# Scaling P on GpSimd ahead of its transpose, swapping the halves of q on GpSimd, and one pool of four 2-bank PSUM tiles

## Chip, cores and metric

The kernel runs on one core of one Trainium2 chip. The metric is the device time of one execution in microseconds (us); lower is better. Before the change it took 650.79 us, the median of 4 runs (650.27 to 651.2).

## The reference, cut to what matters

```python
B, H, S, D = 8, 8, 576, 64
scores = q @ k.T / sqrt(D)                       # per batch and head, 576 x 576
thresh = max(scores, axis=-1) - tau              # tau = 0.02
scores = where(scores >= thresh, scores, -1e9)
attn   = exp(scores - max);  attn /= sum(attn) + 1e-9
x      = (attn @ v) as (B*S, H*D)                # 4608 x 512
h      = max(x @ w1, x @ w2, x @ w3)             # 4608 x 768
out    = h @ w_out                               # 4608 x 512
```

## The kernel before

Work goes in *quads* of four heads, two quads to a batch, 16 in all. A quad is nine *steps*; a step makes two score tiles of 128 queries by 576 keys. In steps 1, 4 and 7 of a quad, counted from 0, the threshold is applied on VectorE, in the others on ScalarE. P is transposed by DMA, and the products for a quad are made in the next quad. Where a batch is complete, its feed-forward is cut into pieces that are slipped between later steps.

```python
ps_s = tc.tile_pool(name="ps_s", bufs=3, space=PSUM)   # 2 banks each: scores, transposes, products
ps_f = tc.tile_pool(name="ps_f", bufs=2, space=PSUM)   # 1 bank each: feed-forward
...
# q transposed; every second use needs it with its two halves of 64 rows swapped:
nc.scalar.activation(out=t, in_=ps[:, 192:768], func=AF.Copy, scale=scale)
nc.gpsimd.dma_start(out=s[0:64], in_=t[64:128])
nc.gpsimd.dma_start(out=s[64:128], in_=t[0:64])
...
def scores(L, idx):                    # both tiles of a step, one after the other
    for i in (1, 0):
        ps = slot("sc")
        for r in (0, 1):               # row half r of the array, its own PSUM bank
            # key columns: i=1: 256 (r=0) and 320 (r=1);  i=0: 320 and 256
            nc.tensor.matmul(ps[:, cols], t[rows, off:off+128], L["kt", pr][rows, kc], ...)
...
def softmax(L, idx, sc):
    nm = -max(sc) (VectorE);  bm = nm + tau
    z  = Exp(sc + nm)  or  Prelu(sc + bm)              # ScalarE, reads PSUM
    P  = z * (z >= thr) (VectorE)  or  Exp(z) (ScalarE), with the row sums
    dma_start_transpose(pt, P)
...
def sums(L):                           # 1/sum of a quad: transpose, DRAM, broadcast back
def product(L, pr, xt):                # P @ v, then times 1/sum on VectorE
def hid(f, a):                         # 3 x 4 matmuls of 288 columns, each evacuated 288 wide
...
for idx in range(9):                   # a step
    fin = softmax(L, idx, sc)
    sc = scores(next step)
    side(g, idx)                       # sums, products, transposes of the next quad's q and k
    if todo: todo.pop(0)()             # one feed-forward piece
    fin()
    if wl and idx >= 2: wl.pop(0)()    # weight loads, in quad 0
```

## Time and profile before

| | before |
|---|---|
| time, median | 650.79 us |
| TensorE (PE) busy | 568.4 us, 87% |
| VectorE (DVE), ScalarE (ACT), GpSimd (POOL) busy | 65%, 60%, 16% |
| first maximum of a score tile | 34.8 us |
| a batch in the steady stretch | 71.4 us |
| from the last reciprocal of the sums to the end | 47.8 us |

The lines of this profile are in the prediction below. In a row of the timeline, the brackets give how long the engine was idle just before and what ended the wait. A chain row gives a start, a length and what took the time.

### The profile page before, as it was taken

What the parts mean: (1) busy time and instruction counts of PE and PEld (TensorE: products, weight loads), DVE (VectorE), ACT (ScalarE), POOL (GpSimd) and SP (SyncE); (2) the same over time, 40 slices, a digit from 0 to 9 for tenths busy, and PEclk for the clock granted to TensorE, in tenths of its full rate; (3) what the DMA queues carried; (4) which work ended last, traced back from release to release, by engine and by line L of the source; (5) the groups of instructions that cost most, each with busy time, mean ns of one, the idle gap of its engine ahead of it and who ended that gap; (6) DMA issues with size and microseconds to landing.
All of it is one profiled execution on the core that took longest, in us unless ns stands there. A gap on an engine that the chain in (4) does not pass through costs nothing.

```text
span 651.5 us, 10435 instructions
## 1 busy us (share of the span) xinstructions
PE 568.4 (87%) x3634; PEld 311.4 (48%) x3648; DVE 423.1 (65%) x880; ACT 389.8 (60%) x841; POOL 105.3 (16%) x194
## 2 busy tenths in 40 slices
PE   3178786999989999999989998999989898999696
PEld 1034333455536553555445553556455553655363
DVE  0055567687667876787767876788668776786141
ACT  1046566666766758576667667675765676676122
POOL 1300111111221012111121112101211021100201
PEclk9999979899999999999999999999999999999899
DMA  8985769776796979796987779685958769574402
GB/s 217 259 196 103 168 143 205 153 172 144 170 220 156 168 132 252 145 190 138 200 198 167 129 171 232 131 197 128 240 124 169 106 112 198 100 121 74 127 1 74
DMA packets 220661, 103.09 MB, mean 158 GB/s; under 512 B 187184, under 2 KB 214208, under 8 KB 220608
## 3 DMA queue, kind: packets, MB, share of 16 engines
q1 hardware_dynamic: 209152, 70.80, 54.7%
q0 software_dynamic: 11456, 31.62, 18.8%
q8 instruction: 29, 0.48, 0.3%
q14 instruction: 24, 0.20, 0.1%
HBM read 44.04 MB, written 9.58 MB: 82 GB/s over the span
## 4 chain that ended last, share of the span: by engine, by line
PE 43%; ACT 24%; DVE 17%; issue 7%; DMA 6%; POOL 0%; SPq 0%; ACTq 0%; POOLq 0%; DVEq 0%
PE sc L155 15%; PE ph L257 13%; ACT P L193 8%; ACT z L182 8%; DVE nm L173 8%; PE tp L124 7%; PE o L232 5%; DVE P L190 4%; DMA qs<-qt 2%; PE po L268 2%; ACT z L180 2%; DMA rb<-rd 2%; ACT qt L128 2%; ACT ob L271 2%; DMA vm<-in_v_dram 2%
## 5 line engine op out<-in xcount | busy, mean ns | idle before, releaser
L173 DVE TENSOR_REDUCE nm<-sc 128x1 f32<-128x576 f32 x288 | 208.6, 752 | 100.3 <-PE sc L155 82.3
L155 PE MATMUL sc<-kt,qs 64*128 64x256 f32 (+1 forms) x512 | 188.9, 473 | 39.4 <-ACT z L182 22.6
L182 ACT ACTIVATE z<-sc,bm 128x576 f32<-128x576 f32 x192 | 134.0, 742 | 122.5 <-DVE bm L176 105.7
L257 PE MATMUL ph<-xt,w 128*128 128x288 bf16 x1152 | 178.1, 289 | 15.2 <-DVE xt L237 5.3
L155 PE MATMUL sc<-kt,qt 64*128 64x256 f32 (+1 forms) x512 | 181.8, 467 | 5.0 <-ACT qt L128 3.0
L257 PEld LDWEIGHTS <-w 128*128 128x128 bf16 x1152 | 107.5, 98 | 77.9 <-issue 49.9
L193 ACT ACTIVATE P<-z 128x576 bf16<-128x576 f32 x192 | 130.0, 690 | 0.0
L155 PEld LDWEIGHTS sc<-kt,qs 64*128 64x128 f32 x512 | 84.6, 197 | 72.9 <-ACT z L182 38.7
L155 PEld LDWEIGHTS sc<-kt,qt 64*128 64x128 f32 x512 | 86.4, 197 | 45.8 <-issue 22.2
L190 DVE SCALAR_TENSOR_TENSOR P<-z 128x576 bf16<-128x576 f32 x96 | 71.4, 753 | 24.8 <-ACT z L180 24.8
L128 ACT ACTIVATE qt<-tp 128x576 f32<-128x576 f32 x32 | 20.8, 651 | 79.8 <-PE tp L124 79.8
L260 ACT ACTIVATE hm<-ph 128x288 bf16<-128x288 f32 x96 | 39.7, 413 | 47.6 <-PE ph L257 47.6
L180 ACT ACTIVATE z<-sc,nm 128x576 f32<-128x576 f32 x96 | 67.2, 751 | 0.0
L262 DVE TENSOR_TENSOR hm<-ph,hm 128x288 bf16<-128x288 f32 x96 | 43.7, 455 | 34.3 <-ACT hm L260 24.6
L268 PE MATMUL po<-wo,hT 128*128 128x512 bf16 (+1 forms) x226 | 56.9, 380 | 1.2 <-ACT ob L271 0.4
L262 DVE TENSOR_TENSOR hT<-ph,hm 128x288 bf16<-128x288 f32 x96 | 43.9, 457 | 13.2 <-PE ph L257 9.2
L130 POOL DMA_DIRECT2D qs<-qt x32 | 16.8, 527 | 195.8 <-ACT hm L260 119.7
L232 PE MATMUL o<-ptq,vb 128*64 128x288 bf16 (+2 forms) x512 | 45.5, 301 | 2.3 <-ACT z L182 2.0
L112 POOL CAST vb<-vm 128x1024 bf16<-128x1024 f32 x16 | 16.7, 1042 | 145.6 <-issue 114.9
L193 ACT ACTIVATION_READ_ACCUMULATOR P<-z 128x1 f32 x192 | 40.0, 208 | 0.0
L274 POOL DMA_DIRECT2D out_dram<-ob x40 | 22.4, 560 | 107.8 <-ACT ob L271 107.5
L134 DVE COPY kt<-tp 128x576 f32<-128x576 f32 x32 | 24.1, 754 | 18.3 <-PE tp L124 18.2
(39 smaller groups left out, 396.9 us busy)
## 6 DMA issues: line engine op xcount, KB each, us to landing
qs<-qt POOLq DMA_DIRECT2D x64, 144.0 KB, 3.3
rb<-rd POOLq DMA_DIRECT2D x32, 288.0 KB, 4.7
qm<-in_q_dram SPq DMA_DIRECT2D x16, 512.0 KB, 5.3
km<-in_k_dram SPq DMA_DIRECT2D x16, 512.0 KB, 5.2
vm<-in_v_dram SPq DMA_DIRECT2D x16, 512.0 KB, 4.2
out_dram<-ob POOLq DMA_DIRECT2D x32, 256.0 KB, 3.8
w<-in_moe_w_dram POOLq DMA_DIRECT2D x3, 768.0 KB, 10.8
ptq<-P SPq DMA_TRANSPOSE x144, 3.4
```

Of the source, the lines that this page charges most:

```text
L124: nc.tensor.transpose(ps[:, col:col + np_], src.rearrange("p a d -> p (a d)"), identf[:np_, :np_])
L155: nc.tensor.matmul(ps[:, cols], t[rows, off:off + 128], L["kt", pr][rows, kc], start=True, stop=True)
L173: nc.vector.tensor_reduce(out=nm[:, n:n + 1], in_=sc[n], axis=AX, op=OP.max, negate=True)
L180: nc.scalar.activation(out=zn, in_=sc[n], func=AF.Exp, bias=nm[:, n:n + 1])
L182: nc.scalar.activation(out=zn, in_=sc[n], func=AF.Prelu, bias=bm[:, n:n + 1], alpha=-STEEP)
L190: nc.vector.scalar_tensor_tensor(out=pn, in0=zn, scalar=thr, in1=zn, op0=OP.is_ge, op1=OP.mult, accum_out=acc)
L193: nc.scalar.activation(out=pn, in_=zn, func=AF.Exp, accum_out=acc)
L232: nc.tensor.matmul(ps[64 * i:64 * i + 64, first + a:first + e], w, x, start=(m == 0), stop=(m == 4))
L257: nc.tensor.matmul(ps[:, :n], wts[wi][:, kc, f * 128:(f + 1) * 128], xt[:, kc, cols], start=(kc == 0), stop=(kc == 3))
L260: nc.scalar.activation(out=hm, in_=ps[:, :n], func=AF.Copy)
L262: nc.vector.tensor_tensor(out=hm if wi == 1 else hT[:, f, cols], in0=ps[:, :n], in1=hm, op=OP.max)
L268: nc.tensor.matmul(ps[:r, :], hT[:, f, c * 128:c * 128 + r], wo[:, f, :], start=(f == 0), stop=(f == NF - 1))
```

## The change

Its intent: (1) multiply P by 1/sum before it is transposed, on idle GpSimd, so that sums need no trip through DRAM; (2) swap the halves of q by GpSimd copies instead of transfers; (3) one pool of four 2-bank PSUM slots for everything, score tiles and other pieces in turn, and the hidden pieces evacuated 576 wide. Weight loads are cut up and begin later in quad 0, the first input loads are split, and outputs leave over the sync queue. The change also gives z a fourth buffer, casts v later, and keeps GpSimd's instructions in the order in which they are written.

```diff
-    ps_s = ctx.enter_context(tc.tile_pool(name="ps_s", bufs=3, space=PSUM))
-    ps_f = ctx.enter_context(tc.tile_pool(name="ps_f", bufs=2, space=PSUM))
+    ps_s = ctx.enter_context(tc.tile_pool(name="ps_s", bufs=4, space=PSUM))
...
-            nc.gpsimd.dma_start(out=s[0:64], in_=t[64:128])
-            nc.gpsimd.dma_start(out=s[64:128], in_=t[0:64])
+            pool.tensor_copy(out=s[0:64], in_=t[64:128])
+            pool.tensor_copy(out=s[64:128], in_=t[0:64])
...
+    def normalized(L, idx, z, sm):
+        rs = small.tile([128, 2], F32, name="rs")
+        vector.reciprocal(rs, sm)
         P = pp.tile([128, W], BF16, name="P")
+        for n in range(2):
+            pool.tensor_scalar(out=P[:, n * S:(n + 1) * S], in0=z[:, n * S:(n + 1) * S],
+                               scalar1=rs[:, n:n + 1], scalar2=1.0, op0=OP.mult, op1=OP.mult)
+        nc.sync.dma_start_transpose(out=L["pt"][:, :, idx * 128:(idx + 1) * 128], in_=P)
-    def sums(L):
...                                     (trip through DRAM, and the multiply in product, removed)
-        def hid(f, a):                  # 12 matmuls, three 1-bank tiles
+        def hid(f, wi):                 # 8 matmuls, one 2-bank tile, evacuated 576 wide
...
-        for idx in range(9):            # two score tiles, then the rest
+        for per in range(18):           # one score tile, one other piece
+            idx, i = per // 2, 1 - per % 2
+            exponents(L, idx, i, sc)
+            sc = scores(next tile)
+            ...
+            other(g, per)               # product at 3 and 8, q/k transposes at 10, 12, 14, 16,
+                                        # else a feed-forward piece
+            if wl and (g or per >= 6) and per % 2:
+                wl.pop(0)()             # weights in 18 loads, from period 7 of quad 0
```

## The prediction

> **What bounds the kernel now.** Words first: a *batch* is two *quads* of four heads; a quad is nine steps; a step makes two score tiles of 128x576 and takes maximum, exponent, threshold and sum of each. Each pair of quads is followed by the feed-forward of its batch, cut into pieces between later steps. I read the page's busy line, then the busy table by stage, then the chain that ended last, then the PE timeline of one steady stretch, then the groups.
>
> The page says TensorE is the busy engine:
>
> ```profile
> PE 568.4 (87%) x3634; PEld 311.4 (48%) x3648; DVE 423.1 (65%) x880; ACT 389.8 (60%) x841; POOL 105.3 (16%) x194
> ```
>
> So GpSimd (POOL) is nearly free, and 83 us of 651.5 have no matmul. The stages tell where. The reciprocal-sum transposes (rp, rs) mark quad starts, at 74.7, 106.8 and 139.06; the first maximum is at 34.8 us. Columns: stretch, length, then busy us of PE, PEld, DVE, ACT, POOL, then clock, DMA share, GB/s.
>
> ```profile
> 34.80:74.70 39.90, 30.74 (x109) 15.41 (x108) 21.92 (x43) 23.30 (x49) 3.36 (x6) 1.00 0.68 148
> 74.70:106.83 32.13, 24.25 (x143) 11.75 (x141) 21.45 (x43) 20.41 (x43) 4.93 (x9) 0.89 0.76 165
> 106.83:139.06 32.23, 28.40 (x184) 14.97 (x184) 22.50 (x48) 20.74 (x46) 4.93 (x9) 0.89 0.76 160
> 139.06:603.20 464.14, 438.09 (x2954) 242.59 (x2965) 342.72 (x717) 312.73 (x681) 77.51 (x141) 1.00 0.77 162
> 603.20:651.50 48.30, 36.52 (x224) 20.64 (x223) 13.02 (x29) 10.02 (x22) 5.96 (x11) 0.90 0.21 64
> ```
>
> The time is 34.8 (start) + 39.9 + 32.1 + 32.2 (quads 0, 1, 2) + 464.1 (13 quads of 35.7) + 48.3 (end) = 651.4. Only the 464 us stretch is TensorE's, at 94% busy. The chain shows what holds start and end (start us, length, what):
>
> ```profile
> 17.55 14.89 DMA qs<-qt
> ...
> 59.37 2.29 PE sc L155 x8
> ...
> 128.77 1.17 PE sc L155 x8
> ...
> 606.44 2.32 DMA rd<-rT
> ...
> 609.56 4.66 DMA rb<-rd
> ...
> 644.63 0.61 ACT ob L271
> ```
>
> At the start everything waits 15 us for the half-swapped q (qs), a transfer queued among weight and input loads. At the end the 1/sum goes through DRAM (rd, rb), and 6.2 us still follow the copy of an output piece (ob). The same eight score records take 2.29 us in quad 0 and 1.17 later: TensorE starts at half rate. In the steady stretch the gaps have this form:
>
> ```profile
> 326.11 0.53 PE L155 MATMUL sc<-kt,qs 64*128 64x320 f32 x1 [0.91 <-ACT z L182]
> ...
> 337.33 0.70 PE L155 MATMUL sc<-kt,qs 64*128 64x256 f32 x2 [1.02 <-ACT z L182]
> ```
>
> A score matmul waits until ScalarE has read an older tile: three PSUM slots serve scores, transposes and products.
>
> **What the Trainium skill says.** *TensorE: Matmul & The Clock Gate*, Part 1: the array runs at half clock until an activity window of about 3.4 us is busy, and falls back after an idle one; Part 4: transposes do not count as that activity. The trace agrees: 2.29 against 1.17 us, and 57 to 66 us, dense with alternating scores and transposes, stayed slow, while dense scores from 75.0 to 78.4 were followed by full rate. *GPSIMD Engine Reference*, section 3.1: a one-input loop with at most two operations costs about 1.03 cycles an element at 1.2 GHz. The casts agree:
>
> ```profile
> L112 POOL CAST vb<-vm 128x1024 bf16<-128x1024 f32 x16 | 16.7, 1042 | 145.6 <-issue 114.9
> ...
> L113 POOL CAST vrb<-vr 128x128 bf16<-128x128 f32 x16 | 4.8, 301 | 0.0
> ```
>
> (1042-301)/896 = 0.83 ns an element plus 195 ns. *SBUF — State Buffer*, "Who interferes with whom": a VectorE instruction with two SBUF inputs contends with a GpSimd instruction that reads SBUF. That is the masked threshold (L190, 96 of 753 ns, both inputs z); with GpSimd this idle, the trace cannot show it yet.
>
> **The change, part by part.**
>
> *TensorE.* Its work stays, less the 16 rp transposes. From dense runs of the chain and timeline: a step's scores 1.17 us, four transposes with remainder 0.95, a product 1.71, twelve hidden matmuls 1.82, an output piece 1.46. Per batch 18x1.17 + 8x0.95 + 4x1.71 + 12x1.82 + 5x1.46 = 64.7 us, 32.4 a quad. The steady quad takes 35.7, so at most 3.3 a quad, 43 us in 13 quads, can be won.
>
> *Steady quads.* Now 18 periods a quad, each one score tile and one other piece, in turn, over four 2-bank slots. A score slot is reused after two periods, 2x1.80 = 3.6 us at TensorE's pace. A tile needs 0.58 to be written, 0.75 maximum (L173), 0.17 bias, 0.74 exponent, some 0.15 of handovers: 2.4. So 1.2 us are left for queueing on VectorE and ScalarE, whose single pieces block for about 0.67 us. Periods with a transpose (0.58+0.95, twice 3.06) leave 0.66. Most gaps of 0.9 to 1.0 should close; short ones remain, above all in masked steps, where a period holds maximum, threshold and often an evacuation on VectorE, 3x0.67 = 2.0 us against 1.8. I choose to win half of the 3.3: 34.0 a quad, 442 us, a gain of 22.
>
> *VectorE.* 192 feed-forward maxima of 0.456 become 96 of about 0.75 (-15.6); bias 96 to 192 (+13.5); 144 reciprocals at 0.2 for 16 (+24.5); rT and the 512-wide scaled copy go (-4.3, -10.9): net +7, some 430 us, 26.5 a quad, below 32.4. *ScalarE.* 96 copies of 0.413 become 48 of 0.74 (-4), 16 copies of 0.6 added (+9.6): some 395, 24.7 a quad. *GpSimd.* 288 scalings of 576 at 0.195+0.83x0.576 = 0.67 us (193), 64 swap copies at 0.67 (43), casts 21.5, 18 weight issues at 0.85 (15): 273 us, 17 a quad. Scaling adds about 1.7 us ahead of each transpose; only the end feels it, as the products run 3 and 8 periods into the next quad.
>
> *Start.* No weight load, no qs transfer; loads split so the first two heads land first. Eight issues of about 0.6 us on the queue, 1.15 MB at 200 to 250 GB/s: the last k at about 8 us, its transposes to 9.6, first tile to 10.9, first maximum at about 12 (was 34.8): gain 23.
>
> *Quads 0 and 1.* Without feed-forward they are held by the other engines and by latency. Pipelined records of ScalarE cost 0.63 each (chain), so an unmasked tile costs 1.30 on ScalarE, a masked one 1.42 on VectorE: 12x1.30 + 6x1.42 = 24.1 a quad if nothing overlaps. At half rate TensorE needs 9x2.29 + 4x1.54 = 26.8 in quad 0. I take 26.5 (was 39.9) and, with products and perhaps some slow clock, 27 (was 32.1). Quad 2, half with feed-forward: 9x1.5 + 9x1.87 = 30.3 (was 32.2). Gain 20.
>
> *End.* From the last exponents to the first hidden matmul: reciprocal 0.2, scaling 1.4, transpose about 3.5, second product 1.7, copy 0.8, about 7.6 us, instead of 11.6 (603.6 to 615.2); less cold ramp (5.30 for 24 matmuls where later 3.65); last output issued by the sync queue. 48.3 becomes 42.5.
>
> Sum: 12 + 26.5 + 27 + 30.3 + 442 + 42.5 = 580.3.
>
> **The rivals.** (a) *The slots give nothing*: the shared pool puts feed-forward pieces, which had two banks of their own, into the scores' queue, and the in-order engines pass one wait to the next. For it: VectorE and ScalarE are at 82% and 76% of such a pace. Against: before, three slots served scores in twos. Steady quads stay 35.7: 602 us. (b) *GpSimd is slower than a cast*: two per-partition scalars, or port contention with L190. At 1.2 us a scaling it has 27 us a quad, still hidden; only beyond 1.6 us does it pass TensorE. At 2 us, 16x40 us and the ends: over 690. Only copies and casts are measured here, so I keep a few per cent. (c) *The clock stays slow through quads 0 and 1*: then TensorE needs 27 and 33 us: some 8 us more, 588. (d) *The steady quads reach TensorE's 32.4*: 560.
>
> **Range and chances.** The start and end gains (23 and 6) rest on transfers seen on the chain and are nearly sure; 29 us alone is 4.5%. Quads 0 to 2 give 8 to 25, steady quads -5 to 43. Outer values 560 and 608. Faster by over 2% needs under 637.8: only rival (b), or a wait I do not see, prevents it.
>
> **What would show each step.** Right: first maximum near 12 us; quad pace 33 to 35; TensorE over 95% busy in the steady stretch, gaps before score matmuls mostly under 0.5 us; scalings of 0.6 to 1.1 us; no qs, rd, rb transfer; hidden matmuls 8 us after the last exponent. Wrong: GpSimd over 80% busy or named as releaser of transposes and products; L190's successor well over 0.75 us; score matmuls still waiting about 1 us for exponents; quads 0 or 1 over 32 us at 2.29 a step.

## The result, and the profile after

The changed kernel took **575.19 us** (median of 4 runs, 570.12 to 576.84) against 650.79 (650.27 to 651.2); the ratio is 0.883 (95% interval 0.878 to 0.888). Here and below a ratio is the mean time of one kernel's fast runs over that of the other's in the same rounds, so it is not quite the ratio of the medians quoted. The profiled run spans 568.3 us and belongs to the fastest of the four.

The page's busy line of the changed kernel:

```profile
PE 541.7 (95%) x3619; PEld 280.1 (49%) x3632; DVE 429.6 (76%) x976; ACT 415.8 (73%) x809; POOL 316.0 (56%) x408
```

TensorE's busy time is down by 27 us, its idle time from 83 to 27 us. The busy table by stage (columns as in the prediction), cut at the first maximum and then at the last reciprocal of the sums of quads 0, 1, 2 and 15:

```profile
0.00:12.20 12.20, 8.20 (x30) 5.30 (x32) 1.52 (x2) 2.58 (x3) 3.36 (x10) 1.00 0.70 199
12.20:36.92 24.72, 19.11 (x108) 8.56 (x106) 22.29 (x57) 21.74 (x45) 18.30 (x24) 1.00 1.05 219
36.92:67.30 30.38, 22.99 (x140) 11.78 (x140) 22.00 (x56) 22.32 (x46) 27.04 (x38) 0.83 1.19 239
67.30:95.89 28.59, 25.45 (x173) 13.26 (x174) 23.06 (x57) 23.52 (x48) 21.68 (x30) 0.94 0.95 192
95.89:533.85 437.96, 436.97 (x2953) 221.87 (x2964) 350.45 (x794) 336.67 (x656) 244.14 (x306) 1.00 0.68 139
533.85:568.30 34.45, 29.02 (x219) 19.32 (x219) 10.24 (x15) 9.02 (x15) 1.47 (x2) 0.98 0.24 74
```

| stretch, us | before | predicted | after |
|---|---|---|---|
| to the first maximum | 34.8 | 12 | 12.2 |
| quad 0 | 39.9 | 26.5 | 24.7 |
| quad 1 | 32.1 | 27 | 30.4 |
| quad 2 | 32.2 | 30.3 | 28.6 |
| 13 steady quads | 464.1 | 442 | 438.0 |
| end | 48.3 | 42.5 | 34.4 |
| sum | 651.4 | 580.3 | 568.3 |

(Before is cut as in the prediction, whose cuts are not of one kind: 74.7 and 106.83 are transposes of 1/sum, 139.06 is the end of a reciprocal, and 603.2 lies 0.5 us before the last one. Cut at the reciprocals, like the changed kernel, before has 37.5, 32.8, 33.7, 464.9 and 47.8. Where experiments are compared below, a quad is measured from its first maximum to the next quad's: quads 0 and 1 then last 34.4 and 33.4 us before, 22.7 and 30.4 after. The clock column counts as full any time for which the trace has no clock record: it says 1.00 up to 12.2 us, where eight score records take 2.31 us, half rate.)

In the steady stretch TensorE now idles for 1.0 us in 438. Its timeline, in which each group of score records (sc) is followed by eight hidden matmuls (ph), and no row carries a wait in brackets:

```profile
231.23 0.48 PE L172 MATMUL sc<-kt,qs 64*128 64x256 f32 x1
231.24 0.53 PE L172 MATMUL sc<-kt,qt 64*128 64x320 f32 x1
231.55 0.38 PE L172 MATMUL sc<-kt,qs 64*128 64x256 f32 x1
231.61 0.43 PE L172 MATMUL sc<-kt,qt 64*128 64x320 f32 x1
231.97 1.15 PE L259 MATMUL ph<-xt,w 128*128 128x288 bf16 x8
233.06 0.53 PE L172 MATMUL sc<-kt,qs 64*128 64x320 f32 x1
```

A single tile runs from 231.23 to 231.97, 0.74 us, then a piece of 1.09: a period of 1.83 us.

The chain at the start:

```profile
4.62 3.65 DMA km<-in_k_dram
8.32 1.60 PE tp L143 x5
9.92 2.31 PE sc L172 x8
12.23 1.41 DVE nm L190 x2
```

and at the end:

```profile
535.67 3.27 DMA ptq<-P
...
538.98 0.85 PE o L236 x10
539.83 17.77 PE ph L259 x144
...
557.87 6.34 PE po L272 x28
```

The k loads end the wait at the start, and no swap stands between transposes and scores. At the end all 144 hidden matmuls run in one stretch at 0.123 us each; the same place of the kernel before has the following row eight times, 0.150 each:

```profile
626.38 1.80 PE ph L257 x12
```

Durations of single instructions (ns, min/median/max, then the first and last start in us). The scaling, from the view of tile P of the changed kernel:

```profile
L36 POOL TENSOR_SCALAR P<-z,rs x288: 737/748/1354, 18.3 to 534.9; 128x576 bf16<-128x576 f32 x144
```

The masked threshold, from the view by line of the changed kernel:

```profile
L204 DVE SCALAR_TENSOR_TENSOR z<-z x96: 735/873/1691, 16.6 to 528.8; 128x576 f32<-128x576 f32 x96
```

and of the kernel before:

```profile
L190 DVE SCALAR_TENSOR_TENSOR P<-z x96: 748/750/760, 41.5 to 597.2; 128x576 bf16<-128x576 f32 x96
```

GpSimd's scaling takes 0.83 us on average, and both it and the masked threshold, which reads SBUF twice, now have a long tail that the threshold did not have before. Sorted by overlap in time, the 190 scalings that meet no masked threshold take 0.737 to 0.754 us, and the 98 that meet one take 0.997 on average.

### The profile page after: what moved, and what is told of

The parts are those of the page before. It is cut to its first block, busy times and chain, and to the rows that moved or that the text cites. A ratio compares the mean times of both kernels' runs of the same rounds, so it can differ in the third digit from the quotient of the medians.

```text
span 568.3 us, 10605 instructions
## 1 busy us (share of the span) xinstructions
PE 541.7 (95%) x3619; PEld 280.1 (49%) x3632; DVE 429.6 (76%) x976; ACT 415.8 (73%) x809; POOL 316.0 (56%) x408
## 4 chain that ended last, share of the span: by engine, by line
PE 79%; DVE 8%; ACT 6%; issue 3%; DMA 2%; SPq 1%; POOL 0%; POOLq 0%; ACTq 0%
PE sc L172 28%; PE ph L259 26%; PE tp L143 9%; PE o L236 8%; PE po L272 7%; DVE nm L190 4%; ACT z L207 2%; DVE z L204 2%; ACT z L196 2%; PE sc L177 2%; DMA ptq<-P 2%; ACT ob L275 1%; DMA km<-in_k_dram 1%; ACT xt L243 1%; ACT z L192 0%
## 5 line engine op out<-in xcount | busy, mean ns | idle before, releaser
L36 POOL TENSOR_SCALAR P<-z,rs 128x576 bf16<-128x576 f32 x288 | 236.1, 832 | 191.0 <-DVE rs L211 95.2
L172 PE MATMUL sc<-kt,qs 64*128 64x320 f32 (+1 forms) x512 | 191.9, 459 | 3.1 <-ACT z L192 2.2
L196 ACT ACTIVATE z<-sc,bm 128x576 f32<-128x576 f32 x192 | 140.8, 736 | 68.4 <-DVE bm L195 39.7
L207 ACT ACTIVATE z<-z 128x576 f32<-128x576 f32 x192 | 131.0, 683 | 4.2
L204 DVE SCALAR_TENSOR_TENSOR z<-z 128x576 f32<-128x576 f32 x96 | 84.1, 877 | 17.4 <-ACT z L192 16.3
L172 PEld LDWEIGHTS sc<-kt,qt 64*128 64x128 f32 x512 | 77.6, 188 | 31.2 <-issue 12.2
L36 POOL COPY qs<-qt 64x576 f32<-64x576 f32 x64 | 49.3, 770 | 28.0 <-ACT qt L147 25.3
L266 DVE TENSOR_TENSOR hm<-ph,hm 128x576 bf16<-128x576 f32 x48 | 36.2, 755 | 15.5 <-PE ph L259 12.9
L263 ACT ACTIVATE hm<-ph 128x576 bf16<-128x576 f32 x48 | 31.0, 646 | 19.1 <-PE ph L259 19.1
L266 DVE TENSOR_TENSOR hT<-ph,hm 128x576 bf16<-128x576 f32 x48 | 36.3, 757 | 3.3 <-PE ph L259 1.1
L272 PEld LDWEIGHTS <-hT 128*128 128x128 bf16 (+1 forms) x240 | 21.2, 100 | 34.9 <-issue 14.7
L236 PEld LDWEIGHTS <-vb 128*64 128x64 bf16 x512 | 25.4, 112 | 25.4 <-issue 17.2
L207 ACT ACTIVATION_READ_ACCUMULATOR z<-z 128x1 f32 x192 | 36.5, 190 | 0.0
```

The source lines that it names most:

```text
L36: ins = fn(*a, **kw)
L172: tensor.matmul(ps[:, cols], t[rows, off:off + 128], L["kt", pr][rows, kc], start=True, stop=True)
L196: scalar.activation(out=zn, in_=sc, func=AF.Prelu, bias=bm, alpha=-STEEP)
L204: vector.scalar_tensor_tensor(out=zn, in0=zn, scalar=thr, in1=zn, op0=OP.is_ge, op1=OP.mult, accum_out=acc)
L207: scalar.activation(out=zn, in_=zn, func=AF.Exp, accum_out=acc)
L236: tensor.matmul(ps[64 * i:64 * i + 64, first + a:first + e], w, x, start=(m == 0), stop=(m == 4))
```

## The experiments

All twelve ran beside the kernel before on the same chips. Two give wrong results.

### Start: the swap alone, and the weight loads alone

`b_swap` is the kernel before with:

```diff
-            nc.gpsimd.dma_start(out=s[0:64], in_=t[64:128])
-            nc.gpsimd.dma_start(out=s[64:128], in_=t[0:64])
+            nc.gpsimd.tensor_copy(out=s[0:64], in_=t[64:128])
+            nc.gpsimd.tensor_copy(out=s[64:128], in_=t[0:64])
```

> The kernel before with one part of the change: the half-swap of q by two GpSimd copies instead of two transfers. Theory (the first scores wait for those transfers, which stand behind the loads): the first maximum moves from 34.8 us to about 20.5 us (four copies of 0.67 us after the casts and the weight issue, which end at 17.5 us), quads after it unchanged, time 651 - 14 = 637 us. Rival (the loads, not the swap, set the start): first maximum stays past 30 us and the time within 3 us of 651.

Measured: 644.0 us (643.6 to 645.33), ratio 0.991 (0.986 to 0.995); first maximum at 21.0 us. The start came forward by 13.8 us, as the theory expected, yet the median by 6.8. The traces show what was kept: the reciprocals of the sums come 13.5 us earlier in quad 0 (58.8 for 72.3) and still 13.2 earlier in quad 15 (590.4 for 603.7). Even a new wait in quad 0, for a P buffer whose transpose stands behind loads, costs little against the kernel before: by first maxima quad 0 lasts 35.4 us for 34.4, and quad 1 31.5 for 33.4. The wait in the chain:

```profile
28.89 11.52 DMA ptq<-P
```

The loss is behind all of it. The last output is issued at 633.0 to 633.6 us, 13.9 earlier than before, but the span ends 8.3 us after it, where the thirteen other profiles need 2.9 to 4.0. The records of the program's closing line, which busy times leave out, show what fills these 4.3 us: a record called DRAIN on GpSimd, 8.15 us long, against 3.77 in the kernel before. In this view (`b_swap`, then the kernel before) it is the longest of three, in ns:

```profile
L369 POOLq DRAIN  x3: 51/93/8154, 633.0 to 641.7; - x3
L369 POOLq DRAIN  x3: 51/102/3768, 646.9 to 651.2; - x3
```

`b_wlate` and `b_pool4`, which also end on GpSimd's queue, have 3.75 and 3.76 us. In the changed kernel it is 3.03 us long and starts at 534.2, far from the end. Output transfers land 2.3 to 2.6 us after their issue, so why it lasts longer in `b_swap` stays open. The remaining difference is one of draws: the profiled run of the kernel before took 653.3 us, 2.5 over its median.

`b_wlate` is the kernel before with the weights one quad later:

```diff
-            if wl and idx >= 2:
+            if wl and g >= 1 and idx >= 2:
```

> The kernel before with another part of the change alone: no weight load before quad 1, the swap still by transfers. Theory of the weights in the way: 3.1 MB of weights no longer share the DMA engines with the swap, which lands some 5 to 7 us after its issue at 16 us; first maximum near 24 us, time about 640 us. Rival (the loads of q, k and v of two quads are enough to hold the swap back): first maximum past 30 us, time 648 to 651 us.

Measured: 651.0 us (648.08 to 651.65), ratio 1.000 (0.996 to 1.005); first maximum at 34.9 us. But the edit changed next to nothing in what ran: the four weight loads are issued at 1.3, 16.6, 17.4 and 22.2 us, against 1.3, 16.0, 16.8 and 21.8 before, and the last lands at 40.1 in both. So this run decides between neither theory nor rival; it shows only that this condition in the loop does not set when the weights load. The chain:

```profile
18.17 14.67 DMA qs<-qt
```

`a_swapdma` is the changed kernel with the two transfers back, over the same ordered GpSimd queue.

> The changed kernel with the half-swap of q by two transfers again, weights late and loads split as in the change. Theory (it is GpSimd's copy that frees the start; loads of q, k and v of two quads still stand in the queue): first maximum past 20 us instead of 12.2, time 8 to 15 us longer, 583 to 590 us. Rival (split loads without weights suffice): first maximum at 14 to 16 us, time 577 to 580 us.

Measured: 589.64 us (580.04 to 595.18), ratio 0.899 (0.889 to 0.909). The rival names the start rightly: with the loads split and no weights ahead the first maximum is at 14.9 us, 2.7 us later than with copies. Of its four runs 588.67 and 580.04 count as fast, 590.61 and 595.18 as slow (over 1.5% above the fastest). The fast ones are still 4.8 and 13.5 us over the change's median, where the theory had 8 to 15: in the profiled one the transfers meet the queue one quad later:

```profile
46.33 0.90 PE L172 MATMUL sc<-kt,qs 64*128 64x320 f32 x1 [9.91 <-DMA qs<-qt]
```

Split loads with no weights ahead are thus enough for most of the 22.6 us at the start, and copies alone for 13.8 of them; but in these runs only copies kept the wait from coming back a quad later.

### Steady stretch: slots and order

`b_pool4` is the kernel before with only its PSUM changed:

```diff
-    ps_s = ctx.enter_context(tc.tile_pool(name="ps_s", bufs=3, space=PSUM))
-    ps_f = ctx.enter_context(tc.tile_pool(name="ps_f", bufs=2, space=PSUM))
+    ps_s = ctx.enter_context(tc.tile_pool(name="ps_s", bufs=4, space=PSUM))
...                                     (feed-forward and rp tiles from slot(...), first bank used)
```

> The kernel before with only its PSUM changed: one pool of four 2-bank slots for scores, transposes, products and feed-forward pieces (still 288 wide, one bank used), instead of three such slots and two single banks. Theory A (slots alone close the gaps): a steady batch of 71.4 us falls to 67 to 69 us, and the feed-forward at the end goes from 1.83 us for twelve matmuls to about 1.5 us, in all 615 to 628 us. Theory B (the order of one tile and one piece in turn is what closes them; four slots with a whole step of two tiles do not): a steady batch stays over 70.5 us or grows, time 640 us or more.

`a_slots3` is the changed kernel with `bufs=3`.

> The changed kernel with three 2-bank slots instead of four, order unchanged. If the fourth slot carries the steady gain: a slot comes round after 1.5 periods, 2.75 us, against the 2.4 us that a tile needs plus queueing, so some 0.3 to 0.8 us are lost per period, a steady batch of 67.2 us becomes 78 to 95 us, time 650 us or more. If the order alone carries it: within 8 us of the changed kernel's 575 us. In the trace the difference shows as score or piece matmuls waiting for ScalarE or VectorE.

`a_pair` is the changed kernel with score tiles two by two:

```diff
-            exponents(L, idx, i, sc)
-            if per < 17:
-                sc = scores(L, (per + 1) // 2, 1 - (per + 1) % 2)
+            exponents(L, idx, i, sc[1 - i])
+            if i == 0:
+                if idx < 8:
+                    sc = [scores(L, idx + 1, 1), scores(L, idx + 1, 0)]
...
```

> The changed kernel with its score tiles issued two by two (both tiles of a step, then two other pieces) instead of one by one. Theory (one by one, a tile's two row halves of 256 and 320 columns do not balance, and a pair costs 2 x 0.74 us against 1.17): TensorE's busy time of a steady batch falls from 67.0 to about 63 us. If four slots still cover the waits, a batch takes 64 to 65.5 us and the whole 553 to 562 us. Rival (two tiles at once bring back the slot waits, as in the kernel before with four slots, 69.1 us with 5.4 us idle): a batch of 67.5 to 70 us, time 578 to 600 us. If the pair cost is not the order's doing, busy stays at 67 us.

Measured: `b_pool4` 622.57 us (621.39 to 628.12), ratio 0.959 (0.952 to 0.967). `a_slots3` 605.74 us (604.66 to 607.93), ratio 0.932 (0.928 to 0.937). `a_pair` 572.93 us (572.35 to 575.48), ratio 0.881 (0.876 to 0.886), the same as the change. One steady batch of each, the kernel before, `b_pool4`, `a_slots3`, `a_pair` and the changed kernel, from the table by stretches:

```profile
250.83:322.23 71.40, 67.45 (x454) 37.34 (x456) 52.87 (x110) 48.25 (x106) 12.69 (x23) 1.00 0.83 175
```

```profile
165.80:234.90 69.10, 63.69 (x457) 37.51 (x458) 52.41 (x110) 48.38 (x106) 12.63 (x23) 1.00 0.86 181
```

```profile
173.10:244.80 71.70, 68.44 (x452) 34.72 (x454) 53.90 (x124) 52.60 (x101) 38.16 (x49) 1.00 0.65 141
```

```profile
200.80:268.00 67.20, 62.80 (x455) 36.45 (x455) 52.87 (x124) 51.19 (x102) 37.74 (x48) 1.00 0.70 150
```

```profile
228.40:295.60 67.20, 67.04 (x453) 34.02 (x456) 54.01 (x124) 51.96 (x101) 38.25 (x49) 1.00 0.74 151
```

| a steady batch, us | length | TensorE busy | idle |
|---|---|---|---|
| before: 3 slots and 2 banks, tiles in pairs | 71.4 | 67.45 | 4.0 |
| `b_pool4`: 4 slots, pairs | 69.1 | 63.7 | 5.4 |
| `a_slots3`: 3 slots, one by one | 71.7 | 68.4 | 3.3 |
| `a_pair`: 4 slots, pairs | 67.2 | 62.8 | 4.4 |
| after: 4 slots, one by one | 67.2 | 67.04 | 0.2 |

Four things follow. With three slots, six banks where the kernel before used eight, the new order gives nothing (71.7), so the fourth slot carries the steady gain, 4.5 us a batch; `a_slots3` lost far less than its expectation of 78 to 95 us, whose queueing was guessed too high. With four slots but the old order, part of it is there (69.1): theory A. `a_pair` also has pairs and four slots, but the rest of the change too; what in that is worth the 1.9 us between them was not taken apart. Pairs and single tiles end at the same 67.2 in two different ways: pairs need 4 us less of TensorE, single tiles leave no gaps. (67.2 lies between the two expectations of `a_pair`, so both missed.) And the 4 us are in the scores: rows of that line alone are busy for 25.8 us of the changed kernel's batch and 21.8 of `a_pair`'s. A tile's two row halves have 256 and 320 key columns and the next tile 320 and 256, so two in a row balance, while a lone tile lasts as long as its longer half.

The unequal halves are the smaller part of it, though. In a pair of `a_pair` at 206.47 us, records inside the burst follow each other after 0.21 us (256 columns) and 0.27 us (320), and the burst's two ends add 0.2 us. That gives 2 x 0.27 + 0.2 = 0.74 us for a lone tile and 2 x 0.21 + 2 x 0.27 + 0.2 = 1.16 for a pair, as measured. So of the 0.31 us by which two lone tiles exceed a pair, about 0.12 come from the unequal halves and 0.2 from paying the two ends twice.

`b_pool4` shows one thing more: at its end twelve hidden matmuls take 1.47 us, not 1.80 to 1.83, though still 288 wide. The end of the kernel before had not run at TensorE's pace, but at that of its two single banks. Its quad 0 fell as well, from 34.4 to 25.9 us, by the slots alone. By the ratios this one edit is worth 4.1 of the change's 11.7%.

`a_slots3` has a slow quad 0, too, 28.8 us by first maxima against 22.7. Its chain there has eight score records at half rate at 28 us:

```profile
28.24 2.29 PE sc L172 x8
```

The clock in the table by stretches of `a_slots3` is full from 12.2 to 15.5 us, half from 15.6 to 18.8, full from 19.0 to 25.7 and half from 25.9 to 39.3. So it was set free as early as in the changed kernel, whose scores run at full rate from 14.59 us on, and was lost again, while the changed kernel keeps 1.00 through quad 0. The other seven profiles with four slots in the changed kernel and copies for the swap have 0.92 to 1.00 there and a quad 0 of 22.3 to 22.8 us (that of `a_rb` from a slow run); `a_swapdma`, whose swap stalls it, has 32.9. That TensorE pauses more with three slots and so loses the clock fits all of these, but none of them was made to test it.

### End: 1/sum behind the product again

`a_rb` is the changed kernel with the kernel before's `sums` and multiply, P written in bf16 at once, and the first product at period 6:

```diff
-    O_A, O_B, T_AT = 3, 8, (10, 12, 14, 16)
+    O_A, O_B, T_AT = 6, 8, (10, 12, 14, 16)
...                                     (normalized: only the transpose; sums() at period 0 of the next quad)
```

> The changed kernel with the 1/sum put back behind the product (transpose of sums, trip through DRAM, multiply at evacuation), P written in bf16 at once, first product at period 6 as the trip takes some 8 us. Theory of the prediction (the scaling of P is worth only what it saves at the end): steady batches 67.0 to 67.6 us as TensorE is full, end 41 to 44 us instead of 38.0, time 576 to 581 us; the masked threshold returns to 0.75 us from 0.88. Rival (GpSimd at its limit in quads 0 and 1 costs more than the end saves): quads 0 and 1 together 5 us or more shorter than 52.9, time 572 us or less.

Measured: fast runs 588.86 to 593.76 us, ratio 0.910 (0.904 to 0.916), some 16 us over the change. Its profile fell on a slow run (602.65), so it is not compared stage by stage. What it shows locally is that the broadcast of 1/sum takes 3.6 to 11.3 us to land and that VectorE waited 21.9 us for it in all. Its masked threshold is back at 0.749 us (median; mean 0.777), as expected. Both expectations of the time missed: the scaling on GpSimd is worth more than what the end saves. A likely reason, seen in the slow profile alone, is that without it the products of every quad depend on a transfer of uncertain length; the later first product is another difference. How much of the 16 us lies at the end stays open.

### Quad 1

Quad 1 is the one stretch that was clearly worse than predicted. The chain of the changed kernel there:

```profile
43.96 6.41 DMA ptq<-P
...
50.41 1.41 PE o L236 x9
```

The second half of the second product waits for a transposed P; TensorE is idle for 2.06 us there. The clock had fallen before: it is at 0.50 from 44.75 to 54.85 us, which makes the 0.83 of this stretch. In the 3.4 us ahead of that, TensorE was busy for 1.57. It stood for 2.4 us behind a ScalarE exponent, which waited for VectorE, whose longest masked threshold (1.69 us, two scalings overlap it) runs at 41.19. So the wait for P is not the only loss in this quad. Four runs went after the cause.

`a_late` places the products of quad 0 later:

```diff
-        if g > 0 and per == O_A:
+        a_at, b_at = (8, 17) if g == 1 else (O_A, O_B)
+        if g > 0 and per == a_at:
```

> The changed kernel with the two products of quad 0 placed at periods 8 and 17 of quad 1 instead of 3 and 8; nothing else. Theory (quad 1 takes 30.3 us because its second product, in TensorE's order ahead of scores, waits up to 6.4 us for the last transposes, which stand behind GpSimd's scalings, weight issues and loads): quad 1 falls to 24 to 26 us, no idle of over 3 us and no half clock in it, time 4 to 6 us less, 569 to 571 us. Rival (GpSimd, busy 27 of these 30 us, is the bound itself): quad 1 stays over 29 us, time within 2 us of 575.

Measured: 573.1 us (570.33 to 577.38), ratio 0.882 (0.876 to 0.888): no gain. Quad 1 is 29.5 us and quad 2 now 36.7. The chain says why:

```profile
67.58 15.73 DMA ptq<-P x2
...
83.36 1.42 PE o L236 x10
```

The transposes at the end of quad 1 land even later. The wait did not sit in the place of the product; it moved with it.

`a_wtiny` (wrong) loads 8 columns of w2 and w3 and uses w1 three times:

```diff
-   pool.dma_start(out=t[:, ko, :], in_=w[ko * 128:(ko + 1) * 128, :])
+   pool.dma_start(out=t[:, ko, 0:c], in_=w[ko * 128:(ko + 1) * 128, 0:c])    # c = 8 for w2, w3
...
-   wts[wi][:, kc, f * 128:(f + 1) * 128]
+   wts[0][:, kc, f * 128:(f + 1) * 128]
```

> Wrong result on purpose: the changed kernel with w2 and w3 loaded as 8 columns each (same instructions, same order on GpSimd, about a third of the weight traffic) and w1 used three times in the matmuls. Theory D (quads 1 and 2 are held by the DMA engines, busy share 1.2 and 1.0 there, so that transposes land up to 6 to 16 us late): share falls below 1, quads 1 and 2 together from 59.2 us to 50 to 54, no wait of over 2 us for a transpose, time 566 to 570 us. Rival G (GpSimd, full in quads 0 and 1, issues the transposes late): nothing changes, quads 1 and 2 stay over 57 us.

`a_noscale01` (wrong) writes P at once in quads 0 and 1 and leaves GpSimd's scaling out there:

```diff
+            if L["raw"]:                              # g < 2
+                L["P"] = pp.tile([128, W], BF16, name="P")
...
+        pn = P[:, n * S:(n + 1) * S] if P is not None else zn
```

> Wrong result on purpose: the changed kernel with no scaling of P in quads 0 and 1 (P written in bf16 by the exponents and thresholds, as in the kernel before), all transfers kept. Theory G (GpSimd full): quad 1 falls from 30.3 to 25 to 27 us and quad 2 stays under 30, time 567 to 571 us. Theory D (DMA engines full): the transposes are issued earlier but land no sooner, since the traffic is the same; quads 1 and 2 together stay within 2 us of 59.2, time 573 to 577 us.

`a_wolate` loads the output weight from period 9 of quad 2 on:

```diff
-            if wl and (g or per >= 6) and per % 2:
+            if wl and (len(wl) > NF and (g or per >= 6) or (g, per) >= (2, 9)) and per % 2:
```

> The changed kernel with the six loads of the output weight moved from the end of quad 1 to quad 2 after period 9, right result. If the DMA engines hold quads 1 and 2, 1.6 MB less of about 10 MB before the first feed-forward piece gives back 2 to 4 us: 571 to 573 us. If GpSimd does, six issues of 0.6 us less in quad 1 give at most 3 us as well, so this run is for the gain, not for telling them apart; no gain at all would say that the moved loads only shift the wait.

Measured: `a_wtiny` 572.47 us (571.9 to 574.18), ratio 0.882 (0.879 to 0.884). `a_noscale01` 573.9 us (573.66 to 574.17), ratio 0.883 (0.880 to 0.886). `a_wolate` 574.79 us (572.07 to 575.59), ratio 0.884 (0.881 to 0.886). Quad 1 of `a_wtiny` and of `a_noscale01`:

```profile
34.80:67.50 32.70, 21.91 (x140) 11.10 (x140) 24.67 (x57) 22.41 (x45) 27.20 (x39) 0.90 1.02 186
```

```profile
34.40:67.70 33.30, 23.85 (x144) 12.20 (x144) 20.51 (x48) 22.63 (x48) 8.20 (x15) 0.80 1.07 209
```

Neither cure helps. With GpSimd busy for 8.2 of 33.3 us the wait is still there, so GpSimd's load alone is not the cause. With w2 and w3 all but left out (a third of the bytes of w1 to w3 remains, half of all weights), quad 1 is still 32.7 us and the DMA share 1.02, so the weights alone are not either. `a_wolate` gains nothing: its quads 1 and 2 last 33.3 and 30.4 us. But in `a_noscale01` the freed GpSimd issued its weight loads sooner, so that run does not hold the traffic still as its expectation claimed. What is left is the sync queue's own traffic. The transfer view of the changed kernel, from 15 to 45 us, and below from 300 to 340 us (columns: count, us to landing):

```profile
ptq<-P SPq DMA_TRANSPOSE x9, 6.0
```

```profile
ptq<-P SPq DMA_TRANSPOSE x12, 3.2
```

A transpose lands after 6.0 us early and 3.2 later. Quads 0 and 1 need as many transposes and input loads as later quads, in two thirds to nine tenths of the time. In the changed kernel the sync queue issues from 33.4 to 53.3 us without a pause, and one transpose holds it for 1.5 to 2.9 us, where 1.3 is the median later. No run took that traffic away, so this stays argued, not shown. The profiled quad 1 of the change, 30.4 us, was also a good draw: the profiles of `a_wtiny`, `a_noscale01`, `a_wolate` and `a_pairwo` have 32.7 to 33.3, that of `a_pair` 34.9, and most runs of the change took 574 to 577 us where the profiled one took 570.

### A candidate

`a_pairwo` joins pairs and the late output weight.

> Score tiles in pairs and the late output weight together, right result: a candidate to beat the change. Steady batch 67.1 us as in pairs alone (TensorE 62.7 busy, the rest waits for slots), first quads 2 to 4 us less, 568 to 572 us. If the pairs' steady stretch is as fast as the singles' only by accident of one run, a batch may lie between 66 and 68.

Measured: 573.12 us (571.25 to 577.75), ratio 0.883 (0.880 to 0.887); a steady batch of 67.1 us. It misses its 568 to 572 us and does not beat the change. No version run here beats it by more than the intervals.

## Why the prediction was right

The time lay 5 us under the predicted 580 and well in the range. The profiled run, the fastest, lies 12 us under the sum, with errors of both signs; by the prediction's own steps:

- **Start**: 12.2 us for 12, right in mechanism and size. `b_swap` and `a_swapdma` showed that the copies, and the split loads with no weights ahead, each reach most of it, so the gain can't be put down to one of them.
- **Quad 0**: 24.7 for 26.5. The step took half rate for granted; scores ran at full rate from 14.59 us on. It also put the old quad 0 down to other engines and latency, while the slots alone took it from 34.4 to 25.9 us (`b_pool4`).
- **Quad 1**: 30.4 for 27. The step that failed is "only the end feels it, as the products run 3 and 8 periods into the next quad": in quad 1 the second product does wait for transposes. `a_late`, `a_wtiny` and `a_noscale01` show that no single one of placing, weights and scalings explains it: without the scalings the wait stays, so it is the slack of 3 and 8 periods that was too small. The clock that the step allowed for fell too, but after a stretch with 1.57 of 3.4 us busy, not after an idle one, as the prediction's rule would have it.
- **Quad 2**: 28.6 for 30.3; not taken apart.
- **Steady quads**: 33.7 (438.0/13) for 34.0, so near by luck, from errors that cancel. TensorE's need was put at 64.7 us a batch and is 67.2 from start to start. The scores' term, 18 x 1.17 = 21.1, was read from tiles issued in pairs and measures 26.1 for single tiles; the hidden term, 12 x 1.82 = 21.8, was read under two single banks and measures 19.7. The gaps were put at 1.6 us a quad and are 0.1.
- **End**: 34.4 for 42.5, the largest miss in size. The chain of copies, transpose and second product was nearly right: the last exponent ends at 533.8 and the first hidden matmul starts at 539.8, 6.0 us for 7.6. The mis-sized term is the hidden matmuls, 1.82 for twelve, taken for TensorE's pace; freed of two single banks they take 1.48, which is 4.1 us over 144. Some 2 us more were not taken apart; outputs over the sync queue, which the prediction had counted on, leave 2.9 us after the last issue for 4.0, as GpSimd's DRAIN is no longer at the end.
- **GpSimd**: 0.83 us a scaling for 0.67. About half of the excess is a scaling slower than the rate of the casts even where no masked threshold overlaps (0.75), half the contention named in advance; hidden in the steady stretch, as predicted.
- **Rivals**: (a) is refuted for four slots; with three, `a_slots3`, the steady batch stays at 71.7 us. (b) did not come: POOL is busy for 56% of the span. (c) came in part, in quad 1. (d) would have needed pairs without gaps.

## What to carry to other kernels

A duration read from a dense stretch belongs to the order and the buffers of that stretch: check whether its neighbours or its PSUM banks set it before it is called an engine's floor. When a slot is added, compare length and busy time together; the same length can hide less work with gaps or more work without. And a wait on a full transfer queue, once removed in one place, is to be looked for one buffer or one quad later. Look at whether an edit changed what ran, too: `b_wlate` moved a condition and hardly a load.

## What the Trainium skill lacked or had wrong

- *TensorE: Matmul & The Clock Gate*, Part 3 (packing by row tiles): it has no word on row halves of unequal length. Here a tile of 256 and 320 columns takes 0.74 us alone and 1.17 in a pair with its mirror; about 0.12 us of the difference of two from a pair come from the unequal halves, 0.2 from the ends of a burst.
- *SBUF — State Buffer*, "Who interferes with whom": agrees that a VectorE instruction with two SBUF inputs contends with GpSimd, but gives no time for such a mix. Here the threshold's mean went from 0.753 to 0.877 us (at most 1.69), and a scaling takes 0.75 us where it meets none and 0.997 on average where it does.
- *GPSIMD Engine Reference*, section 3.1: its rate for up to two operations, 1.03 cycles an element, with 1.2 GHz and a fixed 0.2 us from the casts, gives an estimate of 0.69 us for 576 elements; the section has no fixed time of an instruction in ns. Scalings with a scalar for each partition took 0.737 to 0.754 us where they met no masked threshold.
